# T5 attention and a squared-ReLU FFN on one core: fp32 loads with casts on GpSimd in place of casting loads, and the sums of layer 2's weights on GpSimd in place of VectorE

## The chip, the core and the metric

The kernel runs on one core of a Trainium2 chip. A core has TensorE (matmuls), ScalarE (activations), VectorE and GpSimd (elementwise work), SyncE (here it only issues transfers), and 16 DMA engines that all queues share. The metric is the device time of one execution in microseconds; a lower time is better. The time before is 379.99 us, the median of three runs (378.57 to 380.06).

## The reference

Eight batches, eight heads, 576 positions, head size 64. Attention with a bias that depends on the distance of query and key alone, then an FFN without biases whose activation is the square of a ReLU:

```python
scores = scale * np.matmul(q, k.transpose(0, 1, 3, 2))
scores = scores + bias.transpose(2, 0, 1)[None, :, :, :]
attn = np.exp(scores - np.max(scores, axis=-1, keepdims=True))
attn = attn / (np.sum(attn, axis=-1, keepdims=True) + 1e-09)
attn_out = np.matmul(attn, v)
x = attn_out.transpose(0, 2, 1, 3).reshape(B * S, H * D)      # 4608 x 512
h = np.maximum(x @ w_in, 0.0)                                  # 4608 x 2048
return (h * h @ w_out).astype(np.float32)                      # 4608 x 512
```

All inputs and the output are fp32; the kernel computes in fp16 with fp32 sums in PSUM.

## The kernel before

**Attention.** The unit is a pair of heads: 32 pairs, four for each batch. For a pair, q and k (576 x 128 each) are loaded into a staging buffer, turned so that the head dimension lies on partitions (`qts`, `kts`), and multiplied into scores of four tiles of 128 keys (L628) and two smaller products for the last 64 queries (L652) and the last 64 keys (L677). ScalarE takes the exponentials (L639, L662, L687), VectorE multiplies the bands near the diagonal by a table of exponentials of the bias (L720), TensorE multiplies with v (L756, L763), VectorE normalises (L780, L785) into `x`. For the small products 64 x 64 corners of `qts` and `kts` are copied (L610), mostly by GpSimd.

**Turning.** In batches 0 to 3 (`DT_QK = 4`) TensorE turns q and k (L583): the load put six consecutive rows on each of 96 partitions, and a tile takes 12 transposes of 96 x 96. From batch 4 on the rows lie 128 to a tile and SyncE's queue issues DMA transposes (L566). `x` is turned on TensorE in batches 0 and 1 (`DT_X = 2`, L823) and by DMA transposes (L801) after that.

**FFN.** The 4608 rows of x are nine groups of 512. Layer 1 (L1012) fills 16 tiles of 128 features; a ReLU (L1033 on ScalarE, L1035 on VectorE) and a square (L1043) follow. Layer 2 is a Strassen scheme of seven products (L934) over quarters. It needs sums of the activations (L896, VectorE, each group) and sums of the weights: four for each half, eight in all, made once (`sums_of_weights`, L876, on VectorE).

**Loads.** q, k, v and both weights are loaded on GpSimd's queue by transfers that cast fp32 to fp16 on the way (L261). `load_six` is one transfer of 192 rows of 1536 bytes for a pair's q or k (batches below `SIX = 4`); `load_rows` is three transfers of 512, 512 and 128 rows of 256 bytes; v takes 6 to 10 transfers a batch. Weights are four transfers each, placed among batch 1's loads by `ORDER`.

**What sets the order.** The kernel holds a planner (`Plan`): every operation is an entry with the engines that may run it, an assumed duration, the entries and ring buffers that it depends on, and a due time. `schedule` simulates the engines by these assumed durations, always starting what can start first and is due first, and then emits the instructions in the order of the simulated starts. On the chip each engine, and each issuing queue, then works strictly in that order. Pair p is due at `LEAD + FAST * p` for the first pairs and every `PERIOD` after them; group g's FFN at `G0 + GP * g`. Buffers are rings: five for staged q and k, four for turned q and k, two for exponentials, three batches of v.

Of the kernel before, what the change touches and what calls it, by code (L numbers as in the profile page):

```python
# [29 lines left out]
DT_QK = 4  # L30
PERIOD, LEAD, FAST, FASTN = 9800.0, 7200.0, 5100.0, 8
AHEAD, G0, GP = 8700.0, 28800.0, 41600.0
DT_X = 2
RELU_DVE = 3
NSTG, NQK, NPT, NV, NX, NGB, NRT, NY = 5, 4, 2, 3, 5, 2, 3, 4
P_ORDER = "1 2 6 5 3 7 4"
P_LAST = "1 6 2 5 7 3 4"
SIX = 4
ORDER = "q0 i0 q1 i1 k0 v k1 i2 o0 o1 i3 o2 o3"
# [17 lines left out]
class Ring:  # L57
    def __init__(self, n):
        self.free = [(0.0, i) for i in range(n)]


class Buf:


    def __init__(self, ring):
        self.ring, self.left, self.slot, self.until = ring, 0, None, 0.0

# [20 lines left out]
class Plan:  # L88
# [11 lines left out]
    def schedule(self):  # L100
# [12 lines left out]
        while len(done) < len(self.ops):  # L113
# [24 lines left out]
            for b in op.bufs:  # L138
                if b.slot is None:
                    t, b.slot = min(b.ring.free)  # L140
                    b.ring.free.remove((t, b.slot))
                b.left -= 1
                b.until = max(b.until, op.end + LAT[e])
                if not b.left:
                    b.ring.free.append((b.until, b.slot))
# [13 lines left out]
    @staticmethod  # L159
    def _buf_time(op):  # L160
        t, taken = 0.0, {}
        for b in op.bufs:
            if b.slot is None:
                i = taken[b.ring] = taken.get(b.ring, -1) + 1
                if len(b.ring.free) <= i:
                    return float("inf")
                t = max(t, sorted(b.ring.free)[i][0])
        return t


def mm(n):
    return n / 2.4 + 2.5
# [11 lines left out]
def kernel(  # L184
# [48 lines left out]
    vas = [sb(f"va{i}", [128, 4, H, VW]) for i in range(NV)]  # L233
    v4s = [sb(f"vm{i}", [128, 4, 2, VW]) for i in range(NV)]
# [15 lines left out]
    r_stg, r_qk, r_pt, r_v, r_x = Ring(NSTG), Ring(NQK), Ring(NPT), Ring(NV), Ring(NX)  # L250
    r_gb, r_rt, r_y, r_r = Ring(NGB), Ring(NRT), Ring(NY), Ring(2)
    r_s = {i: Ring(1) for i in (2, 3, 4)}
# [118 lines left out]
    for i in range(NSTG):  # L371
        for w in range(2):
            first.append(
                P.add(
                    {"DVE": 90.0},
                    lambda i=i, w=w: io(nc.vector.memset(stg[i][w][96:128, 512:640].bitcast(FP32), 0.0)),
                    due=40 + i,
                )
            )
    v_fix = []  # L380
    for i in range(NV):
        v_fix.append(
            [
                P.add({"DVE": 110.0}, lambda i=i: io(nc.vector.memset(vas[i][:, :, :, 64:66], VSC)), due=30 + i),
                P.add({"DVE": 350.0}, lambda i=i: io(nc.vector.memset(v4s[i].bitcast(FP32), 0.0)), due=30 + i),
            ]
        )
        for e in range(2):
            v_fix[i].append(
                P.add(  # L390
                    {"DVE": 90.0},
                    lambda i=i, e=e: io(nc.vector.memset(v4s[i][ds(64 * e, 64), :, e, 64:66], VSC)),
                    [v_fix[i][1]],
                    due=30 + i,
                )
            )
# [4 lines left out]
    b_v = [Buf(r_v) for _ in range(B)]  # L401
# [27 lines left out]

    def load_rows(p, w):  # L430

        b, hp = divmod(p, 4)
        src = (q, k)[w][b, 2 * hp : 2 * hp + 2]
        l_qk[p, w] = [
            load(
                "POOL", nc.gpsimd,
                lambda e=e: rows(stg[b_stg[p].slot][w])[:, 0:4, ds(64 * e, D)],
                const(src[e, 0:512, :].rearrange("(t p) d -> p t d", p=128)),
                512 * 34.5, first, [b_stg[p]], pdue(),
            )  # L440
            for e in range(2)
        ] + [
            load(
                "POOL", nc.gpsimd,
                lambda: stg[b_stg[p].slot][w][0:64, 512:640].rearrange("p (e d) -> p e d", e=2),
                const(src[:, 512:S, :].rearrange("e p d -> p e d")),
                128 * 34.5, first, [b_stg[p]], pdue(),
            )
        ]

    def load_v_head(b, h):
        l = load(
            "POOL", nc.gpsimd,
            lambda: vas[b_v[b].slot][:, :, h, 0:64],
            const(v[b, h, 0:512, :].rearrange("(t p) d -> p t d", p=128)),
            512 * 34.5, v_all, [b_v[b]], pdue(),
        )
        l_v.setdefault((b, h // 2), []).append(l)

    def load_v_tail(b):  # L460
        for e in range(2):
            l = load(
                "POOL", nc.gpsimd,
                lambda e=e: v4s[b_v[b].slot][ds(64 * e, 64), :, e, 0:64],
                const(v[b, e::2, 512:576, :].transpose([1, 0, 2])),
                256 * 34.5, v_all, [b_v[b]], pdue(),
            )
            for hp in range(4):
                l_v.setdefault((b, hp), []).append(l)

    def load_v(b):
        for tt in range(4):
            l = load(
                "POOL", nc.gpsimd,
                lambda tt=tt: vas[b_v[b].slot][:, tt, :, 0:64],
                const(v[b, :, ts(tt, 128), :].transpose([1, 0, 2])),
                1024 * 34.5, v_all, [b_v[b]], pdue(),
            )
            for hp in range(4):
                l_v.setdefault((b, hp), []).append(l)  # L480
        load_v_tail(b)

    v_all = v_fix[0] + v_fix[1] + v_fix[2]
# [22 lines left out]
    for hp in range(4):  # L506
        for w in range(2):
            load_six(hp, w)
        if hp == 1:
            load_v_tail(0)  # L510
        if hp >= 1:
            for h in range(2 * hp - 2, 2 * hp):
                load_v_head(0, h)
    for h in range(6, 8):
        load_v_head(0, h)
    for step in ORDER.split():
# [4 lines left out]
        elif step[0] in "qk":  # L521
            for p in range(4 + 2 * int(step[1]), 6 + 2 * int(step[1])):
                load_six(p, "qk".index(step[0]))
        else:
            load_v(1)
    for b in range(2, B):
# [3 lines left out]
        load_v(b)  # L530
# [24 lines left out]
    def pair(p):  # L555
# [5 lines left out]
        for w, dst in ((0, qts), (1, kts)):  # L561
            if b >= DT_QK:
# [7 lines left out]
                    l_qk[p, w], [qb, b_stg[p]], T - 6000, after,  # L570
# [175 lines left out]
        for part, qt0, nq in ((0, 0, 3), (1, 3, 2)):  # L746
            bank = Buf(r_pv)

            def pv(qt0=qt0, nq=nq, bank=bank):
                ps = pv_ps[bank.slot][:, 0 : nq * 130].rearrange("p (t e d) -> p t e d", t=nq, e=2)  # L750
                pt, pm = pts[pb.slot], p4s[pb.slot]
                va, vm = vas[b_v[b].slot], v4s[b_v[b].slot]
                for i in range(nq):
# [3 lines left out]
                            ps[:, i, :, :], pm[:, c : c + 128], vm[:, hp, :, 0:65], start=True, stop=False  # L757
                        )
                    )
                    for e in range(2):  # L760
                        for jt in range(4):
# [4 lines left out]
                                    va[:, jt, 2 * hp + e, 0:65],  # L766
# [7 lines left out]
                bands + list(exps.values()) + l_v[b, hp] + first, [bank, pb, b_v[b]], T + 1, after, "f",  # L774
# [84 lines left out]
    def sums_of_weights():  # L859

        done = []
        for c0 in (0, 4):
# [5 lines left out]
            for out_, a, b_, op in (  # L868
# [6 lines left out]
                    {"DVE": dve(1024, 2.0)},  # L875
                    lambda out_=out_, a=a, b_=b_, op=op: io(nc.vector.tensor_tensor(out=out_, in0=a, in1=b_, op=op)),  # L876
# [117 lines left out]
    def layers(g):  # L994
# [27 lines left out]
        for i in range(16):  # L1022
            if i < len(atoms1):
                nt, f1, bank = atoms1[i]
                o = P.add(
                    {"PE": 4 * mm(512)}, f1, xt_ready[g] + [l_win[nt // 4]], [bank], due + i * 2000, 0.0, "f"
# [80 lines left out]
```

The softmax here doesn't subtract the row's maximum and nothing guards it: scores larger than these inputs give would overflow.

## Time and profile before

| What | Value |
|---|---|
| Runs | 380.06, 378.57, 379.99 us |
| Profiled execution: its time / its span | 379.08 us / 377.1 us |
| TensorE matmul busy | 360.3 us (96%) |
| VectorE / ScalarE / GpSimd busy | 270.3 / 256.6 / 170.1 us |
| Granted TensorE clock | 1.0 throughout |
| Cast queue (GpSimd): packets, share of 16 engines | 86976, 59.4% |
| SyncE's queue: packets, share of 16 engines | 48576, 25.4% |
| L583, transposes of q and k on TensorE | 384 matmuls |
| L876, sums of layer 2's weights on VectorE | 8 of 0.68 to 0.69 us |

The span is the time from the first to the last instruction; the execution's own time is 1.98 us longer. Lines of groups give busy time and the mean duration of one; "idle before" is the time that the engine stood still just before these instructions, with what ended it. The chain of work that ended last is followed back from the last instruction: an engine with a large share of it sets the time.

### The profile page before, as it was taken

The page shows a single profiled execution, that of the slowest core. Times are in us where ns is not written, and L with a number is a line of the kernel's source. Part 1 is how long each engine was busy: PE and PEld are TensorE (multiplying, and loading weights), DVE is VectorE, ACT ScalarE, POOL GpSimd, SP SyncE. Part 2 cuts the span into 40 slices and gives each one's busy share as a digit, 9 for nine tenths or more (in the row PEclk, how much of TensorE's full clock was granted, in tenths as well). Part 3 has the DMA queues.
Part 4 walks back from the last instruction along what each step waited for, and adds up shares of the span by engine and source line. Part 5 has one row for each costly group of instructions (what it writes and reads, how often), then busy time and mean ns, then how long its engine had stood idle before and what let it go on. Part 6 is the DMA issues. An engine that isn't in the chain of part 4 may idle for free.

```text
span 377.1 us, 10222 instructions
## 1 busy us (share of the span) xinstructions
PE 360.3 (96%) x4120; PEld 246.2 (65%) x4120; DVE 270.3 (72%) x628; ACT 256.6 (68%) x366; POOL 170.1 (45%) x298
## 2 busy tenths in 40 slices
PE   2879999999999999999999999999999999999985
PEld 1657456745776766777767665766587776666774
DVE  4799798999779657966597569756865593583652
ACT  2799888888768877877876777877756634353320
POOL 7997462773967676636549593553000000000000
PEclk9999999999999999999999999999999999999999
DMA  7999999794999997996999999998201120010103
GB/s 98 146 176 141 191 203 78 104 136 54 67 141 129 135 113 120 103 128 81 112 157 72 169 97 123 115 104 105 82 21 47 47 75 28 30 56 30 56 34 108
DMA packets 135839, 37.81 MB, mean 100 GB/s; under 512 B 116208, under 2 KB 135792, under 8 KB 135792
## 3 DMA queue, kind: packets, MB, share of 16 engines
q0 software_dynamic: 86976, 18.36, 59.4%
q1 hardware_dynamic: 48576, 18.66, 25.4%
q8 instruction: 32, 0.52, 0.6%
q10 hardware_dynamic: 240, 0.13, 0.2%
q14 instruction: 15, 0.12, 0.1%
HBM read 36.87 MB, written 9.44 MB: 123 GB/s over the span
## 4 chain that ended last, share of the span: by engine, by line
PE 87%; DVE 6%; ACT 3%; DMA 2%; issue 1%; POOL 0%; ACTq 0%; DVEq 0%; POOLq 0%
PE f L1012 34%; PE f L934 28%; PE pv L763 9%; PE st L628 8%; PE pv L756 2%; ACT pt L639 2%; PE st L677 2%; PE st L652 2%; DMA ks<-in_k_dram 2%; PE f L583 1%; DVE pt L720 1%; DVE s L896 1%; PE f L332 1%; DVE x L785 1%; ACT pt L662 0%
## 5 line engine op out<-in xcount | busy, mean ns | idle before, releaser
L1012 PE MATMUL f<-xt,w_in_sb 128*128 128x512 f16 (+4 forms) x704 | 143.0, 341 | 0.1
L639 ACT ACTIVATE pt<-st 128x1024 f16<-128x1024 f32 x128 | 126.1, 1025 | 22.4 <-PE st L628 22.3
L1033 ACT ACTIVATE rt<-f 128x512 f16<-128x512 f32 x136 | 81.3, 598 | 64.8 <-PE f L1012 62.6
L1043 DVE TENSOR_TENSOR g<-rt 128x512 f16<-128x512 f16 x144 | 60.9, 424 | 51.8 <-ACT rt L1033 50.5
L1012 PEld LDWEIGHTS <-w_in_sb 128*128 128x128 f16 x704 | 62.8, 98 | 49.0 <-issue 8.2
L720 DVE TENSOR_TENSOR pt<-pt,tb_sb 128x512 f16<-128x512 f16 (+2 forms) x96 | 58.2, 621 | 9.4 <-ACT pt L639 8.9
L934 PEld LDWEIGHTS <-g 128*128 128x128 f16 x576 | 54.3, 98 | 14.5 <-issue 5.1
L763 PE MATMUL pv<-va,pt 128*128 128x65 f16 x1280 | 54.8, 193 | 0.7 <-DVE pt L720 0.7
L934 PE MATMUL f<-w_out_sb,g 128*128 128x256 f16 x432 | 54.3, 273 | 0.0
L763 PEld LDWEIGHTS <-pt 128*128 128x128 f16 x1280 | 50.3, 97 | 3.6 <-DVE pt L720 0.8
L934 PEld LDWEIGHTS <-s 128*128 128x128 f16 x432 | 40.6, 98 | 12.7 <-issue 3.8
L261 POOL DMA_DIRECT2D qs<-in_q_dram x64 | 44.7, 712 | 4.7 <-PE f L583 3.2
L261 POOL DMA_DIRECT2D ks<-in_k_dram x64 | 44.4, 707 | 2.9 <-DMA w_out_sb<-in_moe_w_out_dram 1.8
L610 POOL COPY qz<-qt 64x64 f16<-64x64 f16 x55 | 18.8, 344 | 56.0 <-DMA qt<-qs 27.7
L628 PE MATMUL st<-qt,kt 64*128 64x512 f16 x256 | 40.5, 387 | 1.8 <-ACT pt L639 0.5
L959 DVE SCALAR_TENSOR_TENSOR y<-f,y 128x512 f32<-128x512 f32 x45 | 31.0, 689 | 14.7 <-PE f L934 14.2
L934 PE MATMUL f<-wt,s 128*128 128x256 f16 x288 | 37.1, 273 | 1.0 <-DVE s L896 1.0
L756 PE MATMUL pv<-vm,pm 128*128 128x130 f16 x160 | 35.4, 221 | 0.5 <-DVE x L785 0.3
L785 DVE TENSOR_TENSOR x<-pv,r 128x384 f16<-128x384 f32 x64 | 31.4, 490 | 2.0
L610 POOL COPY kz<-kt 64x64 f16<-64x64 f16 x51 | 18.1, 356 | 29.8 <-DMA kt<-ks 18.0
L261 POOL DMA_DIRECT2D va<-in_v_dram x36 | 31.0, 882 | 0.2
L896 DVE TENSOR_TENSOR s<-g 128x1024 f16<-128x1024 f16 x36 | 24.8, 688 | 0.2
(61 smaller groups left out, 303.9 us busy)
## 6 DMA issues: line engine op xcount, KB each, us to landing
out_dram<-y SPq DMA_DIRECT2D x36, 256.0 KB, 2.4
va<-in_v_dram POOLq DMA_DIRECT2D x28, 128.0 KB, 5.7
qs<-in_q_dram POOLq DMA_DIRECT2D x16, 144.0 KB, 5.6
ks<-in_k_dram POOLq DMA_DIRECT2D x16, 144.0 KB, 5.3
w_in_sb<-in_moe_w_in_dram POOLq DMA_DIRECT2D x4, 512.0 KB, 8.7
w_out_sb<-in_moe_w_out_dram POOLq DMA_DIRECT2D x4, 512.0 KB, 11.3
qs<-in_q_dram POOLq DMA_DIRECT2D x32, 64.0 KB, 3.7
ks<-in_k_dram POOLq DMA_DIRECT2D x32, 64.0 KB, 3.3
```

The source lines that it names most:

```text
L261: lambda: io(eng.dma_start(out=out_(), in_=in_())),
L610: io(eng.tensor_copy(out=dst[qb.slot][rw, rw], in_=src[qb.slot][rw, 512:576]))
L628: nc.tensor.matmul(sets_ps[st.slot][:, e, :], kt[rw, ts(jt, 128)], qt[rw, 0:512], start=True, stop=True,)
L639: nc.scalar.activation(out=p5(pts[pb.slot])[:, jt, :, 0:512], in_=sets_ps[st.slot], func=EXPF, scale=SCALE)
L720: io(nc.vector.tensor_tensor(out=a, in0=a, in1=t, op=MULT))
L756: nc.tensor.matmul(ps[:, i, :, :], pm[:, c : c + 128], vm[:, hp, :, 0:65], start=True, stop=False)
L763: nc.tensor.matmul(ps[:, i, e, :], pt[:, (2 * jt + e) * S + c : (2 * jt + e) * S + c + 128], va[:, jt, 2 * hp + e, 0:65], start=False, sto ...
L785: nc.vector.tensor_tensor(out=xs[xb.slot][:, qt0 : qt0 + nq, :].rearrange("p t (e d) -> p t e d", e=2), in0=ps[:, :, :, 0:64], in1=rs[rb.s ...
L934: nc.tensor.matmul(g_ps[bank[bk].slot][:, ts(s_, HALF)], left(c, s_), right(c), start=(c == 0 and s_ == 0 and i in (1, 6, 5, 7)), stop=(c ...
L1012: nc.tensor.matmul(g_ps[bank.slot][:, a:z], w_in_sb[:, kk, ts(nt, 128)], xt_sb[:, kk, c : c + z - a], start=(kk == 0), stop=(kk == 3),)
L1033: io(nc.scalar.activation(out=rts[rb.slot], in_=g_ps[bank.slot], func=RELUF))
L1043: nc.vector.tensor_tensor(out=gs[gb1.slot][:, nt, :], in0=rts[rb.slot], in1=rts[rb.slot], op=MULT)
```

## The change

Loads. q and k (all but batch 0's, since `SIX = 1`) and all of v are now fetched as fp32 by plain transfers on SyncE's queue into a ring of three fp32 buffers (`fs`, 128 x 640), and a copy on GpSimd casts from there into the staging buffer or the v buffers. A fetch is three transfers and one cast for q or k, four transfers and three casts for a pair's v. The first fetch is preceded by a dummy transfer on SyncE's queue that reads pair 0's staged k, so that no fp32 load starts before it has landed. Batch 0's q and k and the weights stay casting loads on GpSimd. v is held for a pair (six buffers) where it was held for a batch (three).

Sums. The eight sums of layer 2's weights are issued on GpSimd; a reload of GpSimd's library stands ahead of the first in the built program.

Where things are turned. `DT_QK` goes from 4 to 3, so batch 3's q and k are turned by DMA; those of batches 1 and 2 are now laid out by rows and take 5 transposes of 128 x 128 a tile. `DT_X` goes from 2 to 3, so batch 2's x is turned on TensorE.

The plan's constants change too (periods, due times, the order of the weights among the loads, the order of layer 2's products), and rings of staged q and k, turned q and k, and v are taken in order.

```diff
-DT_QK = 4
-PERIOD, LEAD, FAST, FASTN = 9800.0, 7200.0, 5100.0, 8
-AHEAD, G0, GP = 8700.0, 28800.0, 41600.0
-DT_X = 2
-RELU_DVE = 3
-NSTG, NQK, NPT, NV, NX, NGB, NRT, NY = 5, 4, 2, 3, 5, 2, 3, 4
-P_ORDER = "1 2 6 5 3 7 4"
+DT_QK = 3
+PERIOD, LEAD, FAST, FASTN = 9500.0, 10000.0, 4500, 6
+AHEAD, G0, GP = 3200.0, 52800.0, 40700.0
+DT_X = 3
+RELU_DVE = 2
+NSTG, NQK, NPT, NV, NX, NGB, NRT, NY, NF = 5, 4, 2, 6, 5, 2, 3, 4, 3
+CAST, CAST_V, CAST_T = 900.0, 760.0, 300.0
+P_ORDER = "1 2 6 5 7 3 4"
 P_LAST = "1 6 2 5 7 3 4"
-SIX = 4
-ORDER = "q0 i0 q1 i1 k0 v k1 i2 o0 o1 i3 o2 o3"
+SIX = 1
+ORDER = "k0 q0 o0 i0 i1 k1 v o1 q1 o2 i2 i3 o3"
...
+    fs = [sb(f"f32{i}", [128, 640], FP32) for i in range(NF)]
...
+    def fetch(dmas, casts, bufs, deps):
+
+        fb = Buf(r_f)
+        deps0 = started
+        if not started:
+
+            o = P.add(
+                {"SP": 430.0},
+                lambda: io(
+                    nc.sync.dma_start(
+                        out=fs[fb.slot][0:1, 0:8].bitcast(FP16), in_=stg[b_stg[0].slot][1][0:1, 0:16]
+                    )
+                ),
+                l_qk[0, 1], [fb, b_stg[0]], pdue(),
+            )
+            started.append(P.add({"DMA": 10.0}, None, [o], [fb, b_stg[0]], -1e9))
+        landed = []
+        for dst, src, packets in dmas:
+            o = P.add(
+                {"SP": 430.0}, lambda dst=dst, src=src: io(nc.sync.dma_start(out=dst(fs[fb.slot]), in_=src)),
+                deps0 + f_fix, [fb] + bufs, pdue(),
+            )
+            landed.append(P.add({"DMA": packets * 19.0 / 16}, None, [o], [fb] + bufs, -1e9))
+        return [
+            P.add(
+                {"POOL": ns},
+                lambda out_=out_, in_=in_: io(nc.gpsimd.tensor_copy(out=out_(), in_=in_(fs[fb.slot]))),
+                landed + deps, [fb] + bufs, pool_due[0],
+            )
+            for out_, in_, ns in casts
+        ]
...
-        l_qk[p, w] = [
-            load(
-                "POOL", nc.gpsimd,
-                lambda e=e: rows(stg[b_stg[p].slot][w])[:, 0:4, ds(64 * e, D)],
-                const(src[e, 0:512, :].rearrange("(t p) d -> p t d", p=128)),
-                512 * 34.5, first, [b_stg[p]], pdue(),
-            )
...
+        l_qk[p, w] = fetch(
+            [
+                (
+                    lambda f, e=e: f[:, 0:512].rearrange("p (t e d) -> p t e d", t=4, e=2)[:, :, e, :],
+                    src[e, 0:512, :].rearrange("(t p) d -> p t d", p=128), 512,
+                )
+                for e in range(2)
+            ] + [
+                (
+                    lambda f: f[0:64, 512:640].rearrange("p (e d) -> p e d", e=2),
+                    src[:, 512:S, :].rearrange("e p d -> p e d"), 128,
+                )
+            ],
+            [(lambda: stg[b_stg[p].slot][w][:, 0:640], lambda f: f, CAST)],
+            [b_stg[p]], [],
+        )
...
                 o = P.add(
-                    {"DVE": dve(1024, 2.0)},
-                    lambda out_=out_, a=a, b_=b_, op=op: io(nc.vector.tensor_tensor(out=out_, in0=a, in1=b_, op=op)),
+                    {"POOL": 2400.0},
+                    lambda out_=out_, a=a, b_=b_, op=op: io(nc.gpsimd.tensor_tensor(out=out_, in0=a, in1=b_, op=op)),
                     l + [o], (), 1e5,
                 )
```

## The prediction

> **What bounds the kernel now.** I read the page's busy times first, then the chain of work that ended last, then stretches of the span, then the first 40 us piece by piece, and last the transfers.
>
> ```profile
> PE 360.3 (96%) x4120; PEld 246.2 (65%) x4120; DVE 270.3 (72%) x628; ACT 256.6 (68%) x366; POOL 170.1 (45%) x298
> PEclk9999999999999999999999999999999999999999
> PE 87%; DVE 6%; ACT 3%; DMA 2%; issue 1%; POOL 0%; ACTq 0%; DVEq 0%; POOLq 0%
> ```
>
> TensorE is busy 96% of the span at full clock and carries 87% of the chain. The stretches (columns: PE, PEld, DVE, ACT and POOL busy us with counts, clock, DMA share, GB/s) show where it is not full:
>
> ```profile
> 0.00:10.00 10.00, 2.46 (x44) 1.65 (x44) 4.62 (x45) 3.28 (x5) 7.88 (x16) 1.00 0.79 101
> 20.00:30.00 10.00, 7.91 (x144) 5.21 (x141) 9.68 (x24) 9.98 (x14) 8.17 (x16) 1.00 1.47 176
> 100.00:120.00 20.00, 20.00 (x256) 13.46 (x255) 16.50 (x36) 16.07 (x23) 15.21 (x25) 1.00 1.54 139
> ```
>
> From 40 us to the tail TensorE has no hole: every us of matmul saved or added there is a us of time. Before 40 us only batch 0's attention exists, ScalarE's exponentials set the pace (9.98 of 10), and a hole there is never made up, since all FFN work waits behind it. So two things decide: TensorE's total, and when pair 4 (the first of batch 1) begins. The chain in order of time, with its start and length:
>
> ```profile
> 2.06 5.92 DMA ks<-in_k_dram
> 14.89 1.70 DVE pt L720 x3
> 18.40 1.94 ACT pt L639 x2
> 35.31 0.69 PE st L628 x4
> ```
>
> k of pair 0 lands at 8.0; pair 0's last bands run at 14.9; pair 4's scores start at 35.3.
>
> The transfers on SyncE's queue beside the cast loads on GpSimd's (issue, median us to landing):
>
> ```profile
> far_sb<-in_bias_table_dram SPq DMA_DIRECT2D x1, 4.0 KB, 5.1
> bt_sb<-in_bias_table_dram SPq DMA_DIRECT2D x2, 1.0 KB, 2.2
> out_dram<-y SPq DMA_DIRECT2D x36, 256.0 KB, 2.4
> qt<-qs SPq DMA_TRANSPOSE x16, 4.4
> w_out_sb<-in_moe_w_out_dram POOLq DMA_DIRECT2D x4, 512.0 KB, 11.3
> ```
>
> A small load that shares the engines with GpSimd's first loads (far_sb, 2.1 us into the span) lands after 5.1 instead of 2.2.
>
> **The change, part by part.** The profiled execution is 379.08 us (span 377.1, 1.98 around it); the median of the runs is 379.99, 0.9 more. The sum is made against 379.1.
>
> 1. TensorE's transposes. q and k of batches 1 to 3 no longer take 12 transposes of 96x96 a tile: 24 of 32 runs go. Two such runs inside full TensorE stood from 92.60 to 93.23 in the timeline, 0.31 each: -7.6. Batches 1 and 2 get 16 runs of 5 128-column transposes; four 512-column matmuls take 0.86, so 0.054 each: +4.3. Batch 2's x is turned on TensorE, 20 more: +1.1. Net -2.2. TensorE's waits also hold 3.7 us put to issue before L583's weight loads, up to 2.8 for 24 runs; the 128-row form should not pay them. Between -2.2 and -5.0 I take -3. Eight fewer copies out of PSUM and eight fewer sums on VectorE (8 x 0.69 = 5.5) are worth nothing: in the list of waits TensorE waits for VectorE 2.5 us in all. Nor are the 172 cast loads that GpSimd no longer issues (some 125 of its 170 us): no matmul waited for GpSimd.
>
> 2. The first loads. In the built order GpSimd issues eight q/k loads, then all eight weight loads with no cast between. SyncE holds its first v load until a dummy copy that waits for pair 0's k (8.0) has landed (about 2, bt_sb): 10.4. Weights issued back to back (35.0 to 38.0) landed 42.7 to 52.9 by their shortest and longest landing, with four gaps, so 2.55 each; a q/k load of 144 KB by its bytes 0.72. Hence the cast queue is full until 8.0 + 6 x 0.72 + 8 x 2.55 = 32.7. One fetch (a q, k or v pair) is 1152 rows of 256 B, 72 for each of 16 DMA engines. Price of a row beside that queue: far_sb has 8 rows an engine and lost 5.1 - 2.0 = 3.1 us: 0.39. By the views of single tiles the slowest output store took 5.3 against 2.1 at best, with 16 rows: 0.20; the slowest transpose 7.4 against 2.6, with 40: 0.12. Nothing lost: 0. At 0.20 a fetch needs 14 us, so v of pairs 0 and 1 lands near 25 and 34, and the rest follows once the weights are in. Pair 4 needs the seventh fetch (v0 to v3, k4, k5, q4): five more at 3 or 4 issues of 0.43 plus gaps, 1.8 us each, 34 + 9 = 43, then landing 2.2 and a cast, transpose and evacuation of about 1 each: 47 or so against 35.3, some of which pair 3's own delay covers. At 0.39 it is 49, at no loss 36. I take +10, nearer the rows that are loads and stores than the transposes; ends +1 and +14. TensorE has nothing else then.
> The Trainium skill, "DMA: Bandwidth & Descriptors", section "Queues, rings and completion order", says that an engine takes turns between its queues by whole packets of some 9 to 17 descriptors. By that rule a fetch would get about every second turn and be in by roughly 20 us, and part 2 would be near +1, the sum 381; the far_sb row (one row for some five of the other queue's) speaks against it.
>
> 3. GpSimd's own queue. A library reload and the first of the eight sums stand between v4's and v5's casts, a second sum ahead of q6's. A sum is 0.69 on VectorE; the 64-column copy is 238 against 178 ns (medians), so 0.9, or 1.85 if GpSimd has no doubled fp16 rate (512 fp32 columns take VectorE 0.69). The reload: no row shows one. Nearest below is ScalarE's table load, 1.3; above, eight 16 KB instruction packets in a row at 1.1 each (32 packets, 0.6% of 16 engines' span), 9. So q6's cast is 3 to 13 us later. q6 is the fifteenth fetch, due near 60 after part 2, when TensorE wants it (50 now, plus 10): no cover but SyncE's early issue. I take +2; ends 0 and +10.
> The Trainium skill, "GPSIMD Engine Reference", section "Instruction dispatch", gives about 6 us for the first call after a load of code; by it this part would be +5 and the sum 393. No run here shows it.
>
> 4. GpSimd against VectorE. A copy that began under a band product lasted as long as it:
>
> ```profile
> 22.72 0.96 DVE L720 TENSOR_TENSOR pt<-pt,tb_sb 128x1536 f16<-128x1536 f16 x1
> 22.75 1.02 POOL L610 COPY qz<-qt 64x64 f16<-64x64 f16 x1
> ```
>
> The two-input products (L720, L1043, L896) are 169 us of VectorE. GpSimd's reading grows from 37 us to about 56 x 0.95 + 32 x 0.75 + 64 x 0.24 + 8 x 1.4 + 37 = 141 (casts of 640 and 512 columns between 0.7 and 1.2 by VectorE's 0.69 for 512 times that 1.34). They would exclude each other nearly always. VectorE's 107 idle us hide most; in 60 to 80 us it has 0.5 per 10 left. Ends 0 and +8; I take +1, as TensorE waits for VectorE 2.5 us now.
>
> 5. SyncE's queue. It gets 296 loads; 40 q/k transposes for 32, 40 x transposes for 48, 36 stores. With 0.43, 1.20, 1.18, 0.37 and gaps of 0.05 to 0.17 that is 127 + 48 + 47 + 13 + 29 = 264 us against 108 plus gaps. A batch costs 40 x 0.48 + 8 x 1.37 + 8 x 1.25 + 4.5 x 0.42 = 42 against the 37 that TensorE needs (pair 12 at 106, pair 28 at 255). Behind a load that waits for a cast stand transposes and stores, and TensorE's scores wait for the former. Loads run up to five pairs ahead and the last batches have none, so most is covered: +1, ends 0 and +15. Ends of the transposes themselves get earlier, as no cast loads share the engines after 35 us; they were not waited for by TensorE.
>
> Sum: 379.1 - 3 + 10 + 2 + 1 + 1 = 390.1 by the profiled execution, 391 against the median.
>
> **The rivals.** (a) *The fp32 loads are not held up.* Then parts 2 and 3 vanish, TensorE is the bound from the same moment and 3 to 5 us are gone: 379.1 - 4 = 375, 376 against the median. For it: transposes shared the engines at 0.12 a row or less, and SyncE's issue is cheap. Against: far_sb, and eight weights placed in front. It decides from where a fetch at 10 to 30 us lands within about 5 us of its issue. (b) *SyncE becomes the bound.* The 5 us by which a batch exceeds TensorE's pace add up over batches 3 to 6 and are not covered: +15 on top of part 2, 405. For it: 42 against 37. Against: stretches without transposes before pair 12. (c) *The two sides cancel*: early loss of 3 or 4 us against the transposes: 380.
>
> **How the numbers follow.** Half a per cent, 1.9 us, is about what this kernel's measurement can tell from none. My forecast (383 to 399) has 0.56, (a) 0.25, (b) 0.12, (c) 0.07. Faster 0.25, same 0.07, slower 0.68. The range goes from (a)'s 373 to (b)'s 406.
>
> **What would show it.** Right: pair 4's scores start 8 to 14 us after 35.3, TensorE's busy share in 10 to 40 us falls, the first fp32 loads take over 10 us to land, the weights land by 35; after that TensorE is full; L583's group shrinks to a third. Part 3: a GpSimd gap of several us ahead of its first sum, and q6's transpose waiting for it. Part 4: L720 and L1043 means above 621 and 424 ns. Wrong: first fp32 loads landing in 3 us (then a), or TensorE waiting for kt and qt at 120 to 260 us (then b), or VectorE at nine tenths throughout with TensorE waiting for its products.

## The result and the profile after

The changed kernel takes 452.79 us (median of 4 runs, 451.06 to 456.17) against 379.59 us before (4 runs, 378.57 to 380.06): 1.194 times, 95% interval 1.187 to 1.202. The forecast of 391 had the sign and little more: 73 us were lost where 11 were expected, and the range ended at 406. The profiled execution is 453.58 us, its span 451.8.

The page of the kernel after: busy time, TensorE's clock and the chain that ended last.

```profile
PE 375.7 (83%) x3932; PEld 253.4 (56%) x3932; DVE 290.5 (64%) x622; ACT 255.1 (56%) x360; POOL 151.6 (34%) x292
...
PEclk9856999698999996799799998989999999999999
...
PE 62%; DMA 15%; DVE 13%; SPq 4%; issue 2%; POOL 2%; ACT 1%; POOLq 0%; ACTq 0%
```

TensorE was 96% busy and carried 87% of the chain; now it is 83% and 62%. Its clock is no longer full throughout, and its matmul time is 15.4 us longer although there are 188 matmuls fewer. The stretches of the kernel after (busy us of PE, PEld, DVE, ACT, POOL with counts, then clock, DMA share, GB/s) show three kinds of hole:

```profile
20.00:30.00 10.00, 2.34 (x29) 1.74 (x28) 1.61 (x6) 1.02 (x1) 1.02 (x3) 0.50 1.22 196
...
60.00:80.00 20.00, 15.52 (x154) 7.98 (x152) 19.69 (x27) 14.04 (x20) 18.67 (x24) 0.99 0.55 123
...
100.00:120.00 20.00, 15.27 (x178) 10.01 (x176) 18.84 (x30) 9.86 (x15) 14.79 (x21) 0.91 0.51 118
...
160.00:180.00 20.00, 9.26 (x115) 6.03 (x113) 6.99 (x16) 7.52 (x11) 6.54 (x14) 0.80 0.58 130
...
200.00:220.00 20.00, 15.07 (x187) 10.86 (x183) 13.18 (x27) 13.12 (x18) 6.14 (x12) 0.99 0.59 135
```

At 20 to 30 us next to nothing computes and only the DMA engines work. At 60 to 120 us VectorE is full. At 160 to 220 us no engine in the row is full, and yet TensorE stands. The start of a pair's first scores in the timeline, before and after, says what each kind cost: pair 4 at 35.2 and 53.6 (18.4 us lost), pair 12 at 106.0 and 135.7 (11.3 more), pair 16 at 141.3 and 189.9 (18.9), pair 28 at 255.1 and 330.6 (26.9), end of the span 377.1 and 451.8 (0.8 won back). Together 74.7, the difference of the spans.

A hole costs more than its length: behind it TensorE runs at half clock for a while. Four matmuls of layer 1 ahead of the hole of 169 to 181 us, where the granted clock is 1.00 (165 to 170 us), and four behind it, where it is 0.50 (175 to 185):

```profile
166.12 1.03 PE L1039 MATMUL f<-xt,w_in_sb 128*128 128x512 f16 x4
...
181.88 1.91 PE L1039 MATMUL f<-xt,w_in_sb 128*128 128x512 f16 x4
```

How much of the 15.4 us reaches the end is not shown.

**The early hole.** The chain of the kernel after in order of time (start, length), and TensorE's timeline in the same stretch:

```profile
12.87 10.76 DMA f<-in_v_dram
23.64 14.56 DMA f<-in_v_dram
...
38.69 2.40 DMA f<-in_k_dram
...
44.37 2.36 DMA f<-in_q_dram
```

```profile
25.08 0.27 PE L783 MATMUL pv<-vm,pm 128*128 128x130 f16 x1 [7.75 <-POOL vm L462]
...
33.79 0.66 PE L704 MATMUL st<-qt,kz 128*128 128x288 f16 x2 [6.37 <-POOL kz L637]
...
51.02 0.45 PE L617 MATMUL f<-id_sb,ks 128*128 128x128 f16 x5
...
53.59 0.61 PE L655 MATMUL st<-qt,kt 64*128 64x512 f16 x4
```

Two fp32 loads of v of 128 KB each, one for pair 0 and one for pair 2, keep the chain for 25 us; later loads take 2.4. TensorE, which works in order, stands 7.75 us at pair 0's products with v and 6.37 us at pair 1's last keys. The second wait is for a corner copy that stands on GpSimd behind pair 1's cast. Pair 4's q is cast at 44.9 and turned at 46.0, yet its scores begin at 53.6: in TensorE's order they stand behind the late products of pairs 2 and 3 and behind the turn of pair 6's k, the ninth fetch (L617 at 51.02).

What the DMA engines moved from 20 to 32 us (packets, MB, share of 16 engines; q0 is GpSimd's casting queue with the weights, q1 SyncE's with the fetches):

```profile
q0 software_dynamic: 1901, 1.89, 92.7%
q1 hardware_dynamic: 1900, 0.46, 29.8%
```

Both queues got the same number of packets. But a packet of the weights is some 1 KB and one of a fetch is a row of 256 B, so four fifths of the bytes went to the weights. At 158 rows a us, the estimate from these counts, a fetch of 1152 rows takes 7.3 us.

**VectorE at 60 to 120 us.** Two groups of the page (count | busy us, mean ns) and the sums' line (duration min/median/max, first and last start):

```profile
L1070 DVE TENSOR_TENSOR g<-rt 128x512 f16<-128x512 f16 x144 | 69.9, 488 | 67.7 <-ACT rt L1060 67.1
...
L747 DVE TENSOR_TENSOR pt<-pt,tb_sb 128x512 f16<-128x512 f16 (+2 forms) x96 | 66.7, 708 | 8.7 <-ACT pt L666 8.4
```

```profile
L903 POOL TENSOR_TENSOR wt<-w_out_sb x4: 2116/2121/2822, 54.1 to 104.7; 128x1024 f16<-128x1024 f16 x4
...
L903 POOLq MODIFY_POOL_CONFIG  x2: 3/6/8, 54.0 to 54.0; - x2
```

The band products went from 621 to 708 ns, the squares from 424 to 488. A sum takes GpSimd 2.12 us, three times VectorE's 0.68 to 0.72. If from every VectorE instruction's time the median of its shape in the kernel before is taken off, 26.1 us are too many: 14.8 under a sum, 13.1 under a cast, and 1.8 too few elsewhere.

**The holes from 160 us on.** The largest of TensorE's waits (us in all, times, longest), then the chain across the longest wait:

```profile
PE st L704 <- POOL kz L637: 35.3, 7, 12.2
```

```profile
178.21 2.59 DMA kt<-ks
180.86 0.23 POOL kz L637
...
181.42 0.66 PE st L704 x2
```

TensorE waits for a corner copy, the copy for a transposed kt, and the transpose was issued at 178.21 only. SyncE's timeline says why (start, length, line, what, count):

```profile
168.90 1.22 SPq L593 DMA_TRANSPOSE qt<-qs  x1
170.21 1.80 SPq L455 DMA_DIRECT2D f<-in_q_dram  x3
172.10 1.75 SPq L455 DMA_DIRECT2D f<-in_k_dram  x3
173.95 1.21 SPq L828 DMA_TRANSPOSE xt<-x  x1
175.26 0.54 SPq L1010 DMA_DIRECT2D out_dram<-y  x1
175.90 2.22 SPq L455 DMA_DIRECT2D f<-in_v_dram  x4
178.21 1.23 SPq L593 DMA_TRANSPOSE kt<-ks  x1
```

One ends and the next begins 0.05 to 0.1 us later: SyncE does nothing but issue, and the transpose comes when its turn comes. From 120 to 340 us no gap between two of its issues is longer than 0.5 us. One form of load on its line (duration min/median/max):

```profile
L455 SPq DMA_DIRECT2D f<-in_k_dram x84: 367/540/1497, 35.7 to 310.1; - x84
```

By the medians of the three tensors a load takes SyncE 0.53 to 0.54 us, not the 0.43 of the prediction. With 40 loads at 0.60 with their gap, 8 transposes of q and k at 1.35, 8 of x at 1.31 and 4.5 stores at 0.55, a batch is 47.8 us of issue. A batch goes in 46.9 (pairs 16 to 28, 140.7 us for three); before it went in 37.9. The transfers themselves are quick, by the list of the kernel after:

```profile
f<-in_v_dram SPq DMA_DIRECT2D x64, 128.0 KB, 2.7
...
qt<-qs SPq DMA_TRANSPOSE x20, 2.6
```

### The profile page after: what moved, and what is told of

Its sections match the earlier page's. It is cut to its first block, busy times and chain, and to the rows that moved or that the text cites. A ratio compares the mean times of both kernels' runs of the same rounds, so it can differ in the third digit from the quotient of the medians.

```text
span 451.8 us, 10296 instructions
## 1 busy us (share of the span) xinstructions
PE 375.7 (83%) x3932; PEld 253.4 (56%) x3932; DVE 290.5 (64%) x622; ACT 255.1 (56%) x360; POOL 151.6 (34%) x292
## 4 chain that ended last, share of the span: by engine, by line
PE 62%; DMA 15%; DVE 13%; SPq 4%; issue 2%; POOL 2%; ACT 1%; POOLq 0%; ACTq 0%
PE f L1039 24%; PE f L961 22%; DMA f<-in_v_dram 6%; PE pv L790 6%; PE st L655 5%; DMA kt<-ks 4%; DVE g L1070 3%; DVE pt L747 2%; SPq L455 2%; PE st L704 2%; PE pv L783 2%; DVE x L812 2%; DVE s L923 2%; PE st L679 1%; DMA xt<-x 1%
## 5 line engine op out<-in xcount | busy, mean ns | idle before, releaser
L1039 PE MATMUL f<-xt,w_in_sb 128*128 128x512 f16 (+4 forms) x704 | 148.9, 348 | 1.3 <-DMA xt<-x 1.3
L1070 DVE TENSOR_TENSOR g<-rt 128x512 f16<-128x512 f16 x144 | 69.9, 488 | 67.7 <-ACT rt L1060 67.1
L1039 PEld LDWEIGHTS <-w_in_sb 128*128 128x128 f16 x704 | 64.6, 100 | 49.1 <-issue 10.7
L747 DVE TENSOR_TENSOR pt<-pt,tb_sb 128x512 f16<-128x512 f16 (+2 forms) x96 | 66.7, 708 | 8.7 <-ACT pt L666 8.4
L790 PE MATMUL pv<-va,pt 128*128 128x65 f16 x1280 | 58.4, 197 | 2.5 <-DVE pt L747 2.5
L704 PE MATMUL st<-qt,kz 128*128 128x288 f16 x64 | 15.0, 320 | 37.6 <-POOL kz L637 35.3
L783 PE MATMUL pv<-vm,pm 128*128 128x130 f16 x160 | 36.2, 226 | 11.0 <-POOL vm L462 7.8
L462 POOL CAST va<-f 128x512 f16<-128x512 f32 x32 | 22.2, 692 | 68.9 <-DMA f<-in_v_dram 67.5
L714 ACT ACTIVATE pm<-st 128x576 f16<-128x576 f32 x32 | 20.8, 650 | 28.8 <-PE st L704 28.8
L462 POOL CAST qs<-f 128x640 f16<-128x640 f32 x28 | 23.9, 855 | 34.8 <-DMA f<-in_q_dram 34.3
L462 POOL CAST ks<-f 128x640 f16<-128x640 f32 x28 | 22.6, 807 | 23.1 <-DMA f<-in_k_dram 22.8
L704 PEld LDWEIGHTS <-kz 128*128 128x128 f16 x64 | 5.3, 102 | 44.7 <-POOL kz L637 38.8
## 6 DMA issues: line engine op xcount, KB each, us to landing
w_out_sb<-in_moe_w_out_dram POOLq DMA_DIRECT2D x4, 512.0 KB, 16.5
w_in_sb<-in_moe_w_in_dram POOLq DMA_DIRECT2D x4, 512.0 KB, 16.5
```

The costliest lines, as they stand in the source:

```text
L462: lambda out_=out_, in_=in_: io(nc.gpsimd.tensor_copy(out=out_(), in_=in_(fs[fb.slot]))),
L747: io(nc.vector.tensor_tensor(out=a, in0=a, in1=t, op=MULT))
L783: nc.tensor.matmul(ps[:, i, :, :], pm[:, c : c + 128], vm[:, :, 0:65], start=True, stop=False)
L790: nc.tensor.matmul(ps[:, i, e, :], pt[:, (2 * jt + e) * S + c : (2 * jt + e) * S + c + 128], va[:, jt, e, 0:65], start=False, stop=(jt == ...
L1039: nc.tensor.matmul(g_ps[bank.slot][:, a:z], w_in_sb[:, kk, ts(nt, 128)], xt_sb[:, kk, c : c + z - a], start=(kk == 0), stop=(kk == 3),)
L1070: nc.vector.tensor_tensor(out=gs[gb1.slot][:, nt, :], in0=rts[rb.slot], in1=rts[rb.slot], op=MULT)
```

## The experiments

The theory after the result: three losses, each with its own place. Until pair 4 the fp32 fetches starve beside the weights' casting loads; from 54 to 120 us the sums on GpSimd hold VectorE up; from 120 us on SyncE's issue queue sets the pace. The rivals were that GpSimd beside VectorE explains all of it, or that the fp32 route is slow by itself. Except where an edit says otherwise, the order of every other instruction on every engine is that of the kernel after. All runs in one table, in us: median, then starts of pairs 4, 12, 16 and 28 and the end of the span in the profiled execution.

| run | median | 4 | 12 | 16 | 28 | end |
|---|---|---|---|---|---|---|
| before | 379.6 | 35.2 | 106.0 | 141.3 | 255.1 | 377.1 |
| after | 452.8 | 53.6 | 135.7 | 189.9 | 330.6 | 451.8 |
| 1 merged loads | 422.4 | 53.2 | 137.2 | 178.8 | 298.9 | 419.2 |
| 2 weights behind pair 3's v | 457.8 | 57.6 | 140.9 | 194.8 | 335.3 | 455.6 |
| 3 casts of 8 columns | 445.3 | 52.3 | 127.7 | 182.9 | 325.0 | 446.3 |
| 4 sums on VectorE | 447.6 | 54.8 | 125.2 | 184.8 | 325.5 | 446.9 |
| 5 weights one at a time | 449.5 | 47.5 | 132.3 | 184.9 | 326.8 | 447.1 |
| 6 edits of 1, 4 and 5 | 405.5 | 47.5 | 120.3 | 162.0 | 282.1 | 402.4 |
| 7 before, sums on GpSimd | 397.3 | 35.6 | 122.9 | 158.2 | 272.0 | 394.8 |
| 8 before, turns of rows | 389.9 | 36.2 | 115.0 | 153.6 | 283.1 | 389.1 |
| 9 corners on VectorE | 467.9 | 55.5 | 140.5 | 195.8 | 346.4 | 466.7 |
| 10 weights behind pair 5's q | 453.6 | 38.3 | 137.3 | 188.4 | 330.0 | 450.3 |
| 11 v loads issued by GpSimd | 432.4 | 56.7 | 144.3 | 188.1 | 309.8 | 430.1 |
| 12 edits of 1, 4, 9 and 10 | 413.5 | 41.8 | 123.4 | 163.9 | 289.6 | 409.9 |
| 13 edits of 1 and 4 | 411.4 | 53.1 | 125.0 | 166.6 | 287.5 | 407.8 |
| 14 edits of 1 and 5 | 417.6 | 49.1 | 132.0 | 173.7 | 295.6 | 415.9 |

### SyncE's queue: runs 1 and 11

Run 1 merges the two heads' loads of a fetch; the edit for v, that for q and k is alike.

```diff
-    lambda f, e=e: f[:, ts(e, 256)].rearrange("p (t d) -> p t d", t=4),
-    v[b, 2 * hp + e, 0:512, :].rearrange("(t p) d -> p t d", p=128), 512,
+    lambda f: f[:, 0:512].rearrange("p (t d) -> p t d", t=8),
+    v[b, 2 * hp : 2 * hp + 2].rearrange("e s d -> (e s) d")[0:1024, :].rearrange(
+        "(t p) d -> p t d", p=128), 512,
...
-    (lambda f, e=e: f[ds(64 * e, 64), 512:576], v[b, 2 * hp + e, 512:S, :], 64)
+    (lambda f: f[:, 512:576], v[b, 2 * hp : 2 * hp + 2].rearrange("e s d -> (e s) d")[1024:1152, :], 64)
```

> The kernel after, with each q or k fetch in two load instructions instead of three and each v fetch in two instead of four: 168 load issues on SyncE instead of 296. Bytes, rows of 256 B, casts and the order of every other instruction stay. What is computed is changed in one place: the second head's rows land 64 rows off (1024 rows from the first head's first row on are taken as eight tiles). Theory (SyncE's issue queue is the bound from 120 to 340 us): a batch loses 16 issues of 0.54 us and a gap, 9.4 us, so pairs 16 to 28 go at TensorE's 38 us a batch instead of 46.9; the end comes 25 to 40 us earlier, 413 to 428. Rival (VectorE and GpSimd keep each other waiting all along): SyncE's queue has slack, the pace stays at 46 to 47, the end moves by under 5 us, 448 to 453.

It took 422.43 us, 30.4 less; the ratio to before is 1.114 (1.110 to 1.118). Up to pair 12 nothing moved (137.2 for 135.7); from 16 to 28 a batch goes in 40.0 us instead of 46.9. The same stretch as above, in the run with merged loads, has TensorE full:

```profile
200.00:220.00 20.00, 20.00 (x263) 15.71 (x260) 12.73 (x29) 15.09 (x21) 8.49 (x21) 1.00 0.75 147
```

Run 11 leaves the loads as they are and takes 112 of them to another engine's queue.

```diff
-    def fetch(dmas, casts, bufs, deps):
+    def fetch(dmas, casts, bufs, deps, queue=nc.sync):
...
-    io(nc.sync.dma_start(out=dst(fs[fb.slot]), in_=src))
+    io(queue.dma_start(out=dst(fs[fb.slot]), in_=src))
...
-            [b_v[p]], v_all,
+            [b_v[p]], v_all, nc.gpsimd if p >= 4 else nc.sync,
```

> The kernel after, with the fp32 loads of v from pair 4 on issued by GpSimd instead of SyncE (112 of SyncE's 296 load issues), same buffers, casts and order; the result is the reference's. Theory (SyncE's issue queue is the bound from 120 to 340 us, whatever takes the issues off it): a batch goes in 38 to 41 us instead of 46.9, the end comes 15 to 35 us earlier, 418 to 438. Rival (merging the loads helped for another reason, by fewer instructions to wait for or fewer in flight): the pace stays at 45 or more, or GpSimd, with some 75 us more to issue, takes SyncE's place: 440 or above.

432.43 us, 20.4 less, with 40.6 us a batch; part is given back before pair 12 (144.3), where GpSimd is now over nine tenths busy. Two ways of taking issues off SyncE give the same pace, with GpSimd's casts left whole: the queue is the bound from 120 us on. In run 1 it is relieved but hardly idle: from 160 to 300 us its instructions still fill nine tenths of the time, so that it may also be what keeps a batch at 40.0 there instead of the 37.9 of the kernel before.

### The sums: runs 4 and 7

Run 4 moves only the sums back, in the same place in the order; run 7 makes the opposite edit in the kernel before.

```diff
-    io(nc.gpsimd.tensor_tensor(out=out_, in0=a, in1=b_, op=op))
+    io(nc.vector.tensor_tensor(out=out_, in0=a, in1=b_, op=op))
```

> The kernel after, with the eight sums of layer 2's weights back on VectorE, at the same place in the order. Theory (GpSimd's 2.12 us sums hold up VectorE's products and the casts queued behind them at 54 to 120 us, where VectorE is full): eight sums of 0.69 us take their place, pair 12 starts 2 to 6 us earlier than 135.7. At the end between 0 and 6 us of it are left, 447 to 453. Rival (the sums are harmless, VectorE's own share grows by 5.5 us): pair 12 starts at 135 to 140 and the end is 452 to 457.

> The kernel before, with only the eight sums of layer 2's weights moved from VectorE to GpSimd, same place in the order. Theory (a sum takes GpSimd 2.12 us, holds up VectorE's products meanwhile and whatever stands behind it on GpSimd): 381 to 386, with products of twice their usual time beside the sums. Rival (VectorE is relieved of 5.5 us and GpSimd had slack): 378.5 to 380.

Run 4: 447.61 us (ratio 1.180, 1.176 to 1.185). Pair 12 gains 10.5 us, more than expected, of which 5 reach the end. Run 7: 397.27 us, ratio 1.047 (1.043 to 1.050): the sums alone cost the kernel before 18 us, far beyond the 381 to 386 expected. The timeline of VectorE and GpSimd in run 7 (line 876 is the sums, 1043 the squares, 720 the bands, 763 the products with v):

```profile
88.44 2.18 POOL L876 TENSOR_TENSOR wt<-w_out_sb 128x1024 f16<-128x1024 f16 x1
88.60 2.32 DVE L1043 TENSOR_TENSOR g<-rt 128x512 f16<-128x512 f16 x1
...
90.84 4.81 DVE L720 TENSOR_TENSOR pt<-pt,tb_sb 128x1536 f16<-128x1536 f16 x1
...
92.65 2.18 POOL L876 TENSOR_TENSOR w_out_sb<-w_out_sb 128x1024 f16<-128x1024 f16 x1
...
95.71 0.48 PE L763 MATMUL pv<-va,pt 128*128 128x65 f16 x7 [5.12 <-DVE pt L720]
```

A square of 0.42 us takes 2.32, as long as the sum; the band product behind it, 1.00 at most in the kernel before, takes 4.81 across the second sum, and TensorE waits 5.12 us for it. VectorE's instructions are 21.2 us too long in this run, by the reckoning above, 18.1 of it under sums. Corner copies are lengthened too, up to 2.86 us; products with an fp32 operand are not: one that meets a sum keeps its 0.56 us.

### The early fetches: runs 2, 5 and 10

The eight weight loads are held back: in a row behind pair 3's v (run 2), one behind each cast from pair 2's v to pair 7's k (run 5), or in twos from pair 5's q on (run 10).

```diff
     for op in P.schedule():
         if op.fn is not None:
+            if op in w_issues:
+                held.append(op)
+                continue
             op.fn()
+            if op in behind:
+                held.pop(0).fn()
```

> The kernel after, with GpSimd's eight weight loads issued behind the casts of pair 3's v instead of ahead of the first cast; nothing else is moved. Theory (the first fp32 fetches starve beside the weights): the first v fetch lands within 6 us of its issue instead of 12, pair 4's scores start at 38 to 45 us instead of 53.6, TensorE's clock stays at 1.00 from 20 to 40 us, and the end comes 8 to 16 us earlier, 437 to 445. Rival (SyncE's queue sets the pace later anyway, so that an early gain is eaten there): pair 4 starts earlier, but pair 16 starts at 187 to 190 as now and the end moves by under 4 us, 449 to 453. Second rival (the fetches are held by the three fp32 buffers and SyncE's issue, not by the weights): pair 4 stays above 50.

> The kernel after, with GpSimd's eight weight loads issued one at a time, each behind the cast of one fetch, from pair 2's v to pair 7's k; nothing else is moved. When all eight went behind pair 3's v, pair 2 started 13 us earlier and pair 4 4 us later: the fetches starved wherever the eight ran in a row. Theory (a fetch waits only for casting loads that are already in the queue): with one weight of 2.5 us in the queue at a time, pair 4 starts at 40 to 47 us instead of 53.6. Some of that is lost to SyncE's queue later: the end comes 4 to 12 us earlier, 441 to 449. Rival (what counts is the sum of casting bytes ahead of pair 4, in any order): pair 4 stays at 50 or above, the end within 4 us of 452.8.

> The kernel after, with the eight weight loads in twos behind the casts of pair 5's q, pair 6's k, pair 7's k and pair 4's v. No weight is in the queue while the fetches run that pair 4 needs. Theory (fetches starve only while casting loads are in flight): the seven fetches up to pair 4's q land at most 3 us apart, and pair 4 starts at 35 to 41 us, as in the kernel before; the FFN starts later instead, and the end is 442 to 450, since most of the gain is given back to the late weights and to SyncE's queue. Rival (the fp32 route itself is slow, by SyncE's issue, three buffers and the casts): pair 4 at 44 or later without any weight beside it.

Run 2 was slower than the kernel after, 457.77 us (ratio 1.211, 1.204 to 1.218), and pair 4 started at 57.6: the number of the second rival, but not for its reason, since the first fetches were quick. GpSimd's timeline in run 2 (in brackets its idle time and what ended it):

```profile
24.50 0.95 POOL L462 CAST va<-f 128x512 f16<-128x512 f32 x1 [2.64 <-DMA f<-in_v_dram]
...
26.09 0.77 POOL L270 DMA_DIRECT2D w_out_sb<-in_moe_w_out_dram  x1
...
38.16 0.72 POOL L462 CAST qs<-f 128x640 f16<-128x640 f32 x1 [3.52 <-DMA f<-in_q_dram]
...
46.47 0.72 POOL L462 CAST qs<-f 128x640 f16<-128x640 f32 x1 [7.11 <-DMA f<-in_q_dram]
...
53.68 0.72 POOL L462 CAST ks<-f 128x640 f16<-128x640 f32 x1 [4.93 <-DMA f<-in_k_dram]
```

The four v fetches are cast by 26.1, but then the weights start, and the fetches of pair 4's q, pair 5's q and pair 6's k come 7 to 8 us apart, as the packet counts above suggest. Pair 4 starts behind the last of the three, not behind its own q. The starving had moved along with the weights. Run 10 shows both sides within 20 us, on GpSimd's timeline again:

```profile
26.77 0.72 POOL L462 CAST ks<-f 128x640 f16<-128x640 f32 x1 [1.70 <-DMA f<-in_k_dram]
...
28.58 0.71 POOL L462 CAST ks<-f 128x640 f16<-128x640 f32 x1
...
29.91 0.81 POOL L462 CAST qs<-f 128x640 f16<-128x640 f32 x1 [0.62 <-DMA f<-in_q_dram]
...
32.65 0.77 POOL L270 DMA_DIRECT2D w_out_sb<-in_moe_w_out_dram  x1
...
45.60 1.30 POOL L462 CAST ks<-f 128x640 f16<-128x640 f32 x1 [7.95 <-DMA f<-in_k_dram]
```

With no casting load in flight the fetches up to pair 4's q follow one another in 1.3 to 4.3 us, and pair 4 starts at 38.3, 15 us earlier than after. Then the weights go out, one fetch keeps GpSimd waiting 7.95 us, and pair 6 starts at 72.2 (69.1 after): the gain is gone, 453.60 us, outside the 442 to 450 expected. Run 5 gained 6.1 us at pair 4 (47.5, just beyond what was expected) and 3.3 at the end (449.49; the interval of its ratio, 1.180 to 1.189, overlaps that of the kernel after). So the fetches starve beside casting loads, wherever these stand; that the fp32 route is slow by itself is refuted. By packets the queues are served alike in run 10 too, 1739 and 1618 from 34 to 46 us; that larger rows would get a fetch a larger share follows from this, but no run tried it.

### Casts and corner copies: runs 3 and 9

```diff
-    io(nc.gpsimd.tensor_copy(out=out_(), in_=in_(fs[fb.slot])))
+    io(nc.gpsimd.tensor_copy(out=few(out_()), in_=few(in_(fs[fb.slot]))))   # 8 columns
```

> The kernel after, with GpSimd's casts cut to 8 columns (the 64 tails of v stay whole); loads, transposes and all else stay. Left out: nearly all of q, k and v never reaches the attention. Theory (SyncE is the bound from 120 us on, and casts cost VectorE only where it is full, before 120): VectorE's products lose part of their lengthening, the end moves by 0 to 6 us, 447 to 453. Rival (GpSimd's casts, by the port or by GpSimd's own time, set the pace): the batches of 46.9 us go to 38 to 42 and the end comes 20 us or more earlier, 433 or below.

445.28 us, 7.5 less, a little beyond what the theory gave and far from the rival. A batch still takes 47.4 us from pair 16 on. VectorE's excess falls from 26.1 to 9.7 us, what is left being the sums. (Buffers filled beforehand put pair 0 back to 16.5 us; by pair 2 all but 1 us of that was caught up.)

```diff
-    eng = nc.vector if o.eng == "DVE" else nc.gpsimd
+    eng = nc.vector
```

> The kernel after, with all 64x64 corner copies (qz, kz) on VectorE instead of partly on GpSimd; the order of everything else stays. Theory (a corner copy stands on GpSimd behind a cast that waits for its fetch, so TensorE's scores of the last keys wait 6.4 us for pair 1's kz at 27 to 34 us, and again at 40 to 50): pair 4 starts 2 to 6 us earlier than 53.6 and the end comes 2 to 7 us earlier, 446 to 451. Rival (the corner copies only show the late fetches and transposes that hold everything up): within 2 us of 452.8, or some us later, since VectorE is full at 60 to 120 us and gets about 12 us more.

467.86 us, 15 more. The largest of TensorE's waits in run 9:

```profile
PE pv L783 <- DVE x L812: 28.8, 12, 6.0
```

The waits for kz on GpSimd became waits for VectorE: the copy now stands on VectorE until SyncE's transpose comes (VectorE waits 58 us in all for qt and kt), with the products behind it. The theory of run 9 had taken the corner copy for the cause; it was only where the late transpose showed.

### Together: runs 6, 12, 13 and 14

> The kernel after with three edits together: the fetches in 168 loads instead of 296, the weights spaced as in the run before this, the eight sums on VectorE. What is computed is changed as in the run with merged loads (the second head's rows land 64 rows off). Theory (three separate losses that add up: the early fetches, the sums at 54 to 136 us, SyncE's queue): 452.8 less 30.4 for the loads, 5 to 10 for the sums, 4 to 12 for the weights gives 400 to 413; with SyncE's queue no longer the bound the earlier gains carry through, so nearer 400. Rival (the casts alone, on GpSimd beside VectorE's products, still cost much): 413 or above. Second rival (with these three gone, nothing of the loss is left): 376 to 385.

> The kernel after with four edits together: 168 merged loads (the second head's rows land 64 rows off), the weights behind pair 5's q as two runs before this, the sums and the corner copies on VectorE. Theory (what is left over the 379.3 of before after three edits, 26 us, is half the early fetches and half GpSimd's queue): 385 to 398. Rival (the casts beside VectorE's products and the long way of a fetch over SyncE, GpSimd and SyncE again keep the rest): 399 to 408.

> The kernel after with merged loads (the second head's rows land 64 rows off) and the sums on VectorE; the weights stay in a row at the front. With SyncE's queue out of the way the sums' price is no longer hidden. Theory (the sums cost their 15 us of lengthened products, of which SyncE's queue hid all but 5): the end comes 9 to 13 us before the 422.4 of merged loads alone, 409 to 413, and the gain of pair 12 (10.5 us without merging) is kept to the end. Rival (the sums cost 5 us in either case): 416 to 419.

> The kernel after with merged loads (the second head's rows land 64 rows off) and the weights spaced, one behind each fetch from pair 2's v on; the sums stay on GpSimd. Theory (the 6 us that pair 4 gains by spacing are kept to the end once SyncE's queue is not the bound): 415 to 418. Rival (the gain is given back to fetches that starve later, as where the weights went behind pair 5): 420 to 424. Together with the two edits (405.5), this and the run before say whether the three losses add.

Merged loads alone gain 30.4 us. On top of them the sums gain 11.0 (411.44; 5.2 without merging) and the spaced weights 4.8 (417.60; 3.3 without); all three 47.3 (405.45, ratio 1.067, 1.060 to 1.074), where the single steps add to 46.2. So the losses add once SyncE's queue is relieved, and the queue hid half of what the sums cost. Run 12, with the corner copies on VectorE and the weights late, was 8 us worse than run 6 and above both its 385 to 398 and the rival's 399 to 408; by run 9 the corner copies are a likely reason, but the weights were moved too, and the two weren't separated. In run 6 25.3 us remain against before: 12.3 up to pair 4, 2.0 to pair 12, 6.4 to pair 16, 6.3 to pair 28, and 1.7 won back in the tail. About 17 us of lengthened VectorE work under casts is in it, and from pair 16 on SyncE issues almost without a gap there too; how much each counts wasn't separated, so the cause of these 25 us stays open.

### The transposes alone: run 8

```diff
-DT_QK = 4
+DT_QK = 3
-DT_X = 2
+DT_X = 3
-SIX = 4
+SIX = 2
```

> The kernel before, with its casting loads, but with the change's transposes as far as they can be had without its fetches: batch 2's q and k are turned by 128-column runs of 5, batch 3's by the DMA engines, and batch 2's x by TensorE. TensorE loses 16 runs of 12 (0.31 us each) and gets 8 runs of 5 and 20 transposes (0.054 each): 5.0 less, 3.2 more. Theory (TensorE is the bound): 1.7 us less, up to 3.6 with the gaps ahead of weight loads, 376 to 378.3. Rival (batch 2 and 3's q and k now come by three casting loads instead of one and SyncE gets 8 more transposes, which hold something up): 379 to 384.

389.85 us, ratio 1.027 (1.024 to 1.030), beyond the rival too. The chain of run 8 has pieces that the kernel before hasn't:

```profile
197.49 5.63 DMA xt<-x
...
284.05 8.54 DMA xt<-x
```

TensorE waits for transposed x, but only 4.9 us in all, half of the loss; where the rest comes from isn't shown. With other settings the plan orders the work anew, and this loss hides what the transposes are worth. It says nothing for or against the 3 us.

## Why the prediction was wrong, part by part

**1, the transposes (-3).** Not shown. Run 8 was no clean measure, and in the kernel after no stretch with these transposes is limited by TensorE alone. The size of the term looks right: a run of five 128-column transposes stood 0.29 us (46.90 to 47.19) for the 0.27 foreseen. L583's group shrank to a quarter, 96 of 384, as 24 of 32 runs say; the "third" among the signs was a slip.

**2, the first loads (+10, ends +1 and +14).** That the fetches are slow beside the weights was right, and the times came close: v of pairs 0 and 1 was put near 25 and 34 and was cast at 23.75 and 31.55, and pair 4's q was put at 45 and was cast at 44.9. In part that was luck. The price of 0.20 us a row was too high: by the packet counts it is 0.10, and the first fetch was late for other reasons (the dummy transfer landed at 12.3 and not at 10.4, and SyncE's queue moved nothing from 12.4 to 16 us). The weights were in at 37.9, not at 32.7. What failed is the path, "Pair 4 needs the seventh fetch" and "TensorE has nothing else then": TensorE works in order, pairs 2 and 3 stood behind the late v of pairs 0 and 1, and pair 4's scores behind them and behind the turn of pair 6's k, the ninth fetch. 18.4 us instead of 10. The rule of the Trainium skill that the prediction weighed ("DMA: Bandwidth & Descriptors", "Queues, rings and completion order": an engine takes turns between its queues by whole packets) agrees with the trace, 1901 packets to 1900, though how many are taken in one turn the trace does not show; the far_sb row, read as one row for some five of the other queue's, was the wrong witness against it.

**3, GpSimd's queue (+2).** The reload, bounded by 1.3 and 9 us, shows in the trace as two configuration instructions of 3 to 8 ns, with the first sum at 54.14 directly after a cast. The Trainium skill ("GPSIMD Engine Reference", "Instruction dispatch") has some 6 us for a first call after a load of code; here nothing of it was seen. The sum is 2.12 us, above my end of 1.85, but its price was not the queue behind it on GpSimd: pair 6's q, whose cast was to come 3 to 13 us later, was cast at 64.96, against 64.09 in run 4 with the sums on VectorE.

**4, GpSimd against VectorE (+1, ends 0 and +8).** The step "VectorE's 107 idle us hide most" failed. The idle time lies elsewhere: the sums stand where VectorE is full, and most of them stop it for nearly their whole length (14.8 us for eight sums of 2.1). By run 13 against run 1 they cost 11.0 us, in the kernel before 18 (run 7). The row that I showed, a copy of 1.02 us inside a product of 0.96, was the right one, read as a rate instead of as a stop.

**5, SyncE's queue (+1, ends 0 and +15).** The largest failure; rival (b) had the mechanism, and the sign that I named for it, TensorE waiting for kt and qt at 120 to 260 us, came by way of their corner copies. Two steps were off. An issue with its gap is 0.60, not 0.48: five of the six us by which a batch is longer, 47.8 for 42. And "loads run up to five pairs ahead [...] so most is covered" was wrong: by 168 us the lead was used up, and each further batch cost its full 9 us. Merging the loads gave back 30.4 us.

Together the loads, the sums and the weights account for 47.3 of the 73 us (run 6); the other 26 are not split among causes.

## What to carry to other kernels

A queue that only issues is an engine with a rate: count its instructions per stage, by the length they have when they stand in a row, and compare with that stage's pace; a lead is used up by a lasting excess. When a load moves to another queue, look at what is in flight beside it and how large its packets are, and follow the late datum through every engine that works in order. An engine that shares something with a full one is priced by the full one's time: idle time elsewhere pays nothing.

## What the runs showed of the hardware

- Beside casting loads with packets of 1 KB, an fp32 load of 512 rows of 256 B took 10.8 and 14.6 us from issue to landing, for 2.7 in the median of that run. The two queues were served packet for packet (1901 and 1900 from 20 to 32 us). Without casting loads whole fetches followed one another in 1.3 to 4.3 us (run 10).
- TensorE's granted clock was 0.50 from 20 to 40 us, with TensorE busy for 2.3 of the first 10 us, and again behind the hole of 169 to 181 us: four matmuls took 1.91 us there, and 1.03 ahead of the hole.
- In run 7 all six two-input fp16 products of VectorE that met a 2.1 us sum on GpSimd ended after it (a square took 2.32 us for 0.42); in the kernel after five of seven did.
- From 120 us on SyncE issued a load of 512 rows of 256 B in 0.54 us and a transpose in 1.2 to 1.3, back to back. At 14 to 33 us, with the weights in flight, a single issue took up to 3.2 us, and up to 6.7 in run 1.
